# Causal attention with routed experts: keys and queries brought in on 64 partitions, high and low parts written in place

## The chip, the cores and the metric

The kernel runs on one core of a Trainium2 chip. The time is the device time of one execution in microseconds (us); the median of three runs before the change is 936.29 us (935.67 to 938.85). The trace is that of one execution.

## The reference

Attention over 8 batches x 8 heads, 576 positions, 64 values a head, followed by a two-level routed mixture of 16 experts:

```python
scores = scale * np.matmul(q, k.transpose(0, 1, 3, 2))
cum = np.cumsum(np.maximum(s, 0.0), axis=-1)
bias = -(cum[:, :, :, None] - cum[:, :, None, :])
scores = np.where(causal, -1e9, scores + np.minimum(bias, 0.0))
attn = softmax(scores)                      # row maximum subtracted
x = np.matmul(attn, v)                      # then (B*S, H*D) = (4608, 512)
g_idx = argmax(x @ w_group);  e_idx = argmax(x @ w_expert[g_idx])
out = g_w * e_w * (relu(x @ w1[g, e]) @ w2[g, e])
```

Everything is float32 to the outside. Inside, a product is made of a rounded "high" part and a "low" part, which is the value minus its high part.

## The kernel before

**Tiles.** The 64 heads are worked in 32 pairs. For a pair p there are three kinds of operand tiles. A raw tile `r` holds keys and queries of both heads, transposed: 128 partitions (64 of head 0, 64 of head 1), then key or query, then 576 positions. `WA` (four of them, in turn) holds the high parts with 64 partitions for the head's values and four more rows: two with the cumulated bias (L179) and two with the negated row maximum, high and low (L248); it has room for both heads side by side in the free dimension. `WB` (five in turn) holds on 128 partitions what the low-part products need: low keys over high keys, high queries over low queries. The constants KA = 0 and QA = 1 pick keys or queries.

**The path of a pair.** `load_raw` brings the raw tile in (576 KB). `split` rounds it on ACT into a staging tile `hl` (L152, 128x576 for keys, then the same for queries); the low parts are a subtraction (L156) on POOL, on DVE for pair 0: two of 64x576 for the keys, straight into WB, and one of 128x576 for the queries, into `hl`. `load_a` copies from `hl` to WA by DMA, once a head (L177), and adds the bias rows (L179); `load_b` copies from `hl` to WB, two DMAs a head (L189, L190). So a pair needs six on-chip copies. For pairs 0 to 2 `place` (L168) writes some of them with ACT instead.

**The loop.** A step works on one head. `rowmax` (letter A) multiplies queries by keys (L214) for the head four steps ahead, and DVE reduces each block to row maxima (L222); when both heads of a pair are done, `shift_rows` (letter T) turns the ten columns of maxima by a transposition on TensorE (L236), and `shifts` (t) makes a negated high and low part of them on DVE (L242, L243), which two DMAs from ACT's queue put into WA (D, L248). `scores` (B) makes two matmuls per block (L269 with WA, L271 with WB); ACT takes exponentials (L279, b); POOL zeroes what lies above the diagonal (L288, e), four selections a head. `av` (C) multiplies by the values (L309) for the head before, and ACT evicts (L313, L316, v). The letters Y, Z, W, K normalise, X, L, M make high and low parts of the finished output (L367, L371), O and o send it out. R steps the router.

**What sets the order.** The order on TensorE, DVE, ACT and POOL is written out by hand: the strings ORDER0 (steps −4 to 0), FIRST (steps 1 and 2) and ORDERS (from step 3) are walked letter by letter. A, B and C issue the numbered piece of that head's work, the other letters pop one entry of a first-in-first-out list. G pops one low part, S one split. `need(k, i)` pops everything of list k up to pair i. The start is by hand on SP too; from step 1 on SP's transfers are placed by the planner. `pre` lists extra calls after the early steps.

**The start.** The sums of s are scanned on DVE into `ch` (L469 to L473) and go to WA by L179. `Router` prepares constants on POOL, and `operands` makes eight conversions on DVE after step −1 (L670 to L678). The expert stage follows attention; its weight tiles take SBUF room that attention's tiles leave.

Of the kernel before, what the change touches and what calls it, by code (L numbers as in the profile page):

```python
# [8 lines left out]
F32 = mybir.dt.float32  # L9
F32R = mybir.dt.float32r  # L10
# [10 lines left out]
P = 128  # L21
# [87 lines left out]
def attention(tc, qk, v, s, wr, xs, st):  # L109
# [3 lines left out]
    with ExitStack() as ctx:  # L113
# [28 lines left out]
        hls, raws = {}, {}  # L142
        def load_raw(p):
            raws[p] = raw.tile([P, 2, S], F32, name=f"r{p}", tag="r", bufs=2)
            nc.sync.dma_start(raws[p], qk[p])

        def split(p, part, later=False):

            if part == 0:
                hls[p] = raw.tile([P, 3, S], F32R, name=f"hl{p}", tag="hl", bufs=3)  # L150
            hl, r = hls[p], raws[p]
            nc.scalar.copy(hl[:, part], r[:, part])  # L152

            def low(h):
                hr = slice(0, P) if part else slice(h * 64, h * 64 + 64)
                (nc.vector if p < 1 else nc.gpsimd).tensor_tensor(  # L156
                    out=hl[:, 2] if part else WB[p % NBB][0:64, KA, h], in0=r[hr, part],
                    in1=hl[hr, part].bitcast(F32), op=ALU.subtract)

            for h in range(1 if part else 2):  # L160
                if later:
                    push("G", p, lambda h=h: low(h))
                else:
                    low(h)

        def place(p, part):

            nc.scalar.copy(*((WA[p][0:64, :, 0, QO:], raws[p][0:64]) if part == 0 else  # L168
                             (WB[p][0:64, QA, 0], raws[p][0:64, 1]) if part == 1 else
                             (WB[p][64:128, KA, 1], raws[p][64:128, 0])))  # L170

        def load_a(p, placed=False):
            w = WA[p % NA]
            hl = hls[p].bitcast(F32)
            for h in range(2):
                if h or not placed:
                    nc.sync.dma_start(w[0:64, :, h, QO:].bitcast(F32), hl[h * 64:h * 64 + 64, 0:2])  # L177
                n = 2 * p + h
                nc.sync.dma_start(w[64:66, KA, h, QO:].bitcast(F32), (cumh if p < 4 else cumd)[n:n + 1].bitcast(F32))  # L179

        def load_b(p, placed=False):
            w = WB[p % NBB].bitcast(F32)
            hl = hls.pop(p).bitcast(F32)
            for h in range(2):

                hr = slice(h * 64, h * 64 + 64)
                b = slice(1 if placed and h else 0, 2)
                if h or not placed:
                    nc.sync.dma_start(w[0:64, QA, h], hl[hr, 1])  # L189
                nc.sync.dma_start(w[64:128, b, h], hl[hr, 0::2][:, b])  # L190
# [41 lines left out]
        def shift_rows(p):  # L232
            need("a", 2 * p + 1)
            i = p % NA
            pt = ring(f"pmt{p}", "t", True)
            nc.tensor.transpose(pt[:10, :P], mc[p % 2], ident)  # L236
            push("t", p, lambda: shifts(p, i, pt))

        def shifts(p, i, pt):
            th = sm.tile([10, P], F32R, name=f"th{p}", tag="th", bufs=1)  # L240
            tl = sm.tile([10, P], F32R, name=f"tl{p}", tag="tl", bufs=1)
            nc.vector.tensor_scalar(out=th, in0=pt[:10, :P], scalar1=-1.0, scalar2=None, op0=ALU.mult)  # L242
            nc.vector.scalar_tensor_tensor(out=tl, in0=pt[:10, :P], scalar=-1.0, in1=th.bitcast(F32), op0=ALU.mult,  # L243
                                           op1=ALU.subtract)
# [214 lines left out]
        load_raw(0)  # L459
        load_raw(1)  # L460
        wr_f = ac.tile([P, 4, 20], F32, name="wr_f")
# [46 lines left out]
        place(2, 1)
        place(2, 2)
# [22 lines left out]
        ORDER0 = "B0 b e A0 a T t B1 b D A1 a B2 b e A2 a B3 b e e A3 a B4 b e A4 a A5 a".split()  # L532
        for step in range(-LEAD, NH + 5):
# [19 lines left out]
            if step >= 2 and step // 2 + 4 < NP:  # L553
                push("S", step // 2 + 4, lambda p=step // 2 + 4, part=step % 2: split(p, part, True))
# [24 lines left out]
            if step % 2 == 1 and 0 < step < NH:  # L579
                for f, lead in ((load_a, 4), (load_b, 3), (load_v, 1), (load_raw, 6)):  # L580
                    if step // 2 + lead < NP and (f != load_v or step > 1):
                        need("S", step // 2 + lead)
                        if f in (load_b, load_raw):
                            need("G", step // 2 + lead - 2 * (f == load_raw))
                        f(step // 2 + lead)
# [39 lines left out]
class Router:  # L625
# [42 lines left out]
    def operands(self):  # L668
        V, ni, n1 = self.tc.nc.vector, self.ni, self.n1
        V.tensor_copy(self.wr_sb[:, :, 0:20], self.wr_f)  # L670
        V.tensor_tensor(out=self.wr_sb[:, :, 32:52], in0=self.wr_f, in1=self.wr_sb[:, :, 0:20].bitcast(F32),
                        op=ALU.subtract)
        V.tensor_copy(self.ub, self.uf)
        V.tensor_copy(self.ob, self.onesf)
        V.tensor_scalar(out=ni, in0=n1, scalar1=6, scalar2=None, op0=ALU.arith_shift_right)
        V.tensor_copy(self.part[:, 0], ni)
        V.tensor_scalar(out=ni, in0=n1, scalar1=63, scalar2=None, op0=ALU.bitwise_and)
        V.tensor_copy(self.part[:, 1], ni)  # L678
# [918 lines left out]
```

## Time and profile before

| | |
|---|---|
| median of three runs | 936.29 us |
| the profiled execution | 940.03 us, span 938.2 us, mean granted TensorE clock 0.981 |
| TensorE matmul busy | 872.6 us (93%) |
| DVE, ACT, POOL busy | 698.0 (74%), 607.6 (65%), 613.8 (65%) |
| DMA over the span | 174.66 MB, 186 GB/s |

Busy shares are means over the whole span: attention fills about the first 440 us, the expert stage the rest. A granted clock of 1.00 is 2.4 GHz, 0.50 is 1.2 GHz. In a timeline row, the number in front is the start in us from the span's begin, the next the duration, and the bracket says how long the engine was idle before and what ended that. A DMA issue stands on the queue (SPq, ACTq) that issues it, and its duration is that of the issue, not of the transfer.

### The profile page before, as it was taken

The numbers are of one execution on the slowest core, as the hardware profiler recorded it, in microseconds if no ns is written. First come the engines' busy times: TensorE is split into PE (matmuls) and PEld (weight loads), VectorE is DVE, ScalarE is ACT, GpSimd is POOL, SyncE is SP. The second block draws the span as 40 slices with busy tenths as digits, with TensorE's granted clock in tenths as the row PEclk, the third lists the DMA queues.
The fourth block names the chain that finished last, engine by engine and source line by source line (L and its number), as shares of the span: only waits on it lengthen the run. The fifth ranks groups of instructions, "written<-read, shape, count | busy, mean of one in ns | idle before, by whom it ended". The sixth has DMA issues, their size and how long they took to land. (4 is left out here: it accounts for less than half of the span.)

```text
span 938.2 us, 17960 instructions
## 1 busy us (share of the span) xinstructions
PE 872.6 (93%) x5648; PEld 783.8 (84%) x5648; DVE 698.0 (74%) x1986; ACT 607.6 (65%) x1382; POOL 613.8 (65%) x731
## 2 busy tenths in 40 slices
PE   4879999999999999999799999999999999999993
PEld 3768788787878788787597999899999999999992
DVE  7536586886868586886477678998888899888830
ACT  5547777776777677766646467566676666766740
POOL 9636665666757565633688556666768778878750
PEclk9979999999999999999799999999999999999997
DMA  6999988788889878733365545455554556655510
GB/s 181 233 183 222 235 221 225 181 220 210 226 197 225 211 211 217 164 98 130 123 210 183 173 162 193 157 195 209 184 189 182 204 188 226 225 203 188 195 44 23
DMA packets 80502, 174.66 MB, mean 186 GB/s; under 512 B 9580, under 2 KB 42988, under 8 KB 72208
## 3 DMA queue, kind: packets, MB, share of 16 engines
q1 hardware_dynamic: 70496, 153.52, 58.3%
q0 software_dynamic: 7488, 18.89, 5.6%
q10 hardware_dynamic: 2416, 1.03, 0.5%
q8 instruction: 47, 0.77, 0.4%
q14 instruction: 55, 0.45, 0.2%
HBM read 108.97 MB, written 19.69 MB: 137 GB/s over the span
## 5 line engine op out<-in xcount | busy, mean ns | idle before, releaser
L995 POOL TENSOR_TENSOR wl<-raw,wh 128x512 fp32r<-128x512 f32 x182 | 233.5, 1304 | 58.2 <-ACT wh L992 39.7
L222 DVE CUSTOM_DVE_ANT_0 mx<-pm,mask 128x192 bf16<-128x192 f32 (+4 forms) x320 | 129.4, 421 | 50.2 <-PE pm L214 46.1
L992 ACT CAST wh<-raw 128x512 fp32r<-128x512 f32 x256 | 153.8, 616 | 3.7 <-issue 3.1
L1093 PE MATMUL ph<-xl,wh 128*128 128x256 f32 (+13 forms) x512 | 145.5, 304 | 4.4 <-DVE xl L1065 4.1
L1093 PE MATMUL ph<-xh,wh 128*128 128x256 f32 (+13 forms) x512 | 144.4, 301 | 1.2 <-ACT xh L1064 1.1
L214 PE MATMUL pm<-WA 66*128 66x288 f32 (+4 forms) x384 | 126.8, 359 | 18.6 <-DMA WA<-ch 9.7
L269 PE MATMUL ps<-WA 68*128 68x320 f32 (+4 forms) x384 | 136.9, 360 | 6.0 <-DVE tl L243 3.0
L309 PE MATMUL po<-pt,VT 128*128 128x256 f32 (+3 forms) x512 | 123.8, 359 | 2.6 <-issue 2.1
L1148 PE MATMUL py<-hl,wh 128*128 128x256 f32 (+13 forms) x448 | 113.5, 302 | 1.3 <-DVE hl L1089 1.3
L1148 PE MATMUL py<-hh,wh 128*128 128x256 f32 (+13 forms) x448 | 112.9, 302 | 0.0
L271 PE MATMUL ps<-WB 128*128 128x320 f32 (+4 forms) x384 | 111.6, 303 | 0.0
L309 PE MATMUL po<-pu,VT 128*128 128x320 f32 (+1 forms) x384 | 108.9, 393 | 0.0
L1194 DVE STREAM_TRANSPOSE yr<-yT 32x384 f32<-32x384 f32 (+1 forms) x208 | 104.4, 502 | 4.2
L288 POOL TENSOR_SCALAR_AFFINE_SELECT pt<-pt 128x128 f32<-128x128 f32 (+2 forms) x192 | 64.2, 343 | 65.0 <-ACT pt L279 62.3
L1060 DVE STREAM_TRANSPOSE xt<-xg 32x256 f32<-32x256 f32 (+1 forms) x208 | 102.4, 493 | 3.2
L1093 PEld LDWEIGHTS ph<-xl,wh 128*128 128x128 f32 x512 | 96.7, 189 | 8.2 <-DVE xl L1065 6.2
L309 PEld LDWEIGHTS po<-pt,VT 128*128 128x128 f32 x512 | 89.0, 195 | 16.7 <-issue 3.3
L1093 PEld LDWEIGHTS ph<-xh,wh 128*128 128x128 f32 x512 | 96.8, 189 | 2.8 <-ACT xh L1064 2.4
L371 POOL TENSOR_TENSOR xTl<-xT,xTh 128x512 fp32r<-128x512 f32 x30 | 38.2, 1272 | 90.9 <-ACT xTh L367 74.3
L214 PEld LDWEIGHTS pm<-WA 66*128 66x128 f32 (+1 forms) x384 | 70.0, 195 | 32.2 <-DVE mc L222 14.9
L1088 ACT ACTIVATE hh<-ph 128x256 fp32r<-128x256 f32 (+13 forms) x128 | 53.6, 419 | 65.1 <-PE ph L1093 64.2
L156 POOL TENSOR_TENSOR WB<-r,hl 64x576 fp32r<-64x576 f32 x62 | 87.2, 1406 | 5.1 <-ACT hl L152 2.6
(230 smaller groups left out, 1994.3 us busy)
## 6 DMA issues: line engine op xcount, KB each, us to landing
raw<-in_w_dram SPq DMA_DIRECT2D x64, 1024.0 KB
r<-in_qk_dram SPq DMA_DIRECT2D x32, 576.0 KB
WA<-hl SPq DMA_DIRECT2D x61, 288.0 KB
WB<-hl SPq DMA_DIRECT2D x61, 288.0 KB
VT<-in_v_dram SPq DMA_DIRECT2D x32, 384.0 KB
WB<-hl SPq DMA_DIRECT2D x64, 144.0 KB
xs<-xr SPq DMA_DIRECT2D x15, 512.0 KB
WA<-cumd SPq DMA_DIRECT2D x56, 4.5 KB
```

The source lines that it names most:

```text
L156: (nc.vector if p < 1 else nc.gpsimd).tensor_tensor(out=hl[:, 2] if part else WB[p % NBB][0:64, KA, h], in0=r[hr, part], in1=hl[hr, part]. ...
L214: nc.tensor.matmul(ps[:rows, :cw], WA[i][0:66, QA, h, QO + q0:QO + q0 + rows], WA[i][0:66, KA, h, QO + c0:QO + c0 + cw], start=True, stop= ...
L222: nc.vector.tensor_tensor_reduce(out=tmp[:rows, :cw], in0=ps[:rows, :cw], in1=mk[:rows], scale=1.0, scalar=-3.0e38 if c0 == 0 else mo, op0 ...
L269: nc.tensor.matmul(ps[:rows, o:o + w], WA[i][0:68, KA, h, QO + k0:QO + k0 + rows], WA[i][0:68, QA, h, QO + q0:QO + q0 + w], start=True, st ...
L271: nc.tensor.matmul(ps[:rows, o:o + w], WB[p % NBB][:, KA, h, k0:k0 + rows], WB[p % NBB][:, QA, h, q0:q0 + w], start=False, stop=True)
L309: nc.tensor.matmul(po[0][:, qa - base:qb - base], VT[p % NVT].rearrange("p t a d -> p (t a d)")[:, (3 * t + 1 + h) * 64:][:, 0:P], x[:, c: ...
L992: self.casts.append(nc.scalar.copy(h[:, j], raw[:, j]))
L995: self.low = nc.gpsimd.tensor_tensor(out=l[:, j], in0=raw[:, j], in1=h[:, j].bitcast(F32), op=ALU.subtract)
L1060: V.transpose(dst[:, 0:n, :, j], src[:, 0:n, :, i])
L1093: self.product = nc.tensor.matmul(pss[f][:, :cap], w[f // 4][:, c, (f % 4) * P:(f % 4 + 1) * P], x[:, c, :cap], start=(c == 0 and w is sel ...
L1148: self.product = nc.tensor.matmul(pss[c][:, :cap], w[2 + f // 4][:, f % 4, c * P:(c + 1) * P], x[:, f, :cap], start=(f == 0 and w is self. ...
L1194: V.transpose(dst[:, 0:n, :, i], src[:, 0:n, :, j])
```

## The change

Keys and queries are laid out in HBM so that a pair's raw tile has 64 partitions, then head, key or query, and position. ACT rounds one head's keys and queries (64x1152) straight into WA; POOL (DVE for pair 0) makes four low parts of 64x576 a pair, straight into WB; two DMAs from WA to WB (288 KB each) give the high parts there. The staging tile and `place` are gone. Raw tiles have three buffers instead of two, and are loaded at even steps behind `need("G")`. The bias rows of both heads come by one DMA from pair 3 on. The ten columns of maxima are copied beside themselves on DVE, twenty are transposed, and the second DVE instruction makes the high part in ten rows and the low part in the other ten by a per-row factor (`less`, 0 or −1), so that one DMA sends them. `operands` is cut into four pieces after steps 1 to 4. Loads of values, of raw tiles and of WB move from odd steps to even ones.

```diff
-        def load_raw(p):
-            raws[p] = raw.tile([P, 2, S], F32, name=f"r{p}", tag="r", bufs=2)
-            nc.sync.dma_start(raws[p], qk[p])
+        def load_raw(p, heads=((0, 2),)):
+            raws[p] = raw.tile([64, 2, 2, S], F32, name=f"r{p}", tag="r", bufs=3)
+            for a, b in heads:
+                nc.sync.dma_start(raws[p][:, a:b], qk[p][:, a:b])
-        def split(p, part, later=False):
...
-            nc.scalar.copy(hl[:, part], r[:, part])
+        def split(p, h, later=False):
+            r, w, wb = raws[p], WA[p % NA], WB[p % NBB]
+            nc.scalar.copy(w[0:64, :, h, QO:], r[:, h])
+            def low(a):
                 (nc.vector if p < 1 else nc.gpsimd).tensor_tensor(
+                    out=wb[64 * a:64 * a + 64, a, h], in0=r[:, h, a], in1=w[0:64, a, h, QO:].bitcast(F32),
+                    op=ALU.subtract)
+            for a in (KA, QA):
                 if later:
+                    push("G", p, lambda a=a: low(a))
...
+        def load_a(p):
             w = WA[p % NA]
+            if p < 3:
...
+            else:
+                nc.sync.dma_start(w[64:66, KA, :, QO:].bitcast(F32), cumd[2 * p:2 * p + 2].rearrange("h a s -> a h s"))
+        def load_b(p):
+            w, wb = WA[p % NA].bitcast(F32), WB[p % NBB].bitcast(F32)
+            nc.sync.dma_start(wb[0:64, QA], w[0:64, QA, :, QO:])
+            nc.sync.dma_start(wb[64:128, KA], w[0:64, KA, :, QO:])
...
+            nc.vector.tensor_copy(mc[p % 2][:, 2 * NB:], mc[p % 2][:, 0:2 * NB])
             pt = ring(f"pmt{p}", "t", True)
-            nc.tensor.transpose(pt[:10, :P], mc[p % 2], ident)
+            nc.tensor.transpose(pt[:20, :P], mc[p % 2], ident)
...
+            nc.vector.scalar_tensor_tensor(out=t, in0=th.bitcast(F32), scalar=less, in1=pt[:20, :P], op0=ALU.mult,
                                            op1=ALU.subtract)
...
+                nc.scalar.dma_start(WA[i][66:68, QA].bitcast(F32).rearrange("a h q -> a (h q)"), t.bitcast(F32))
...
-        load_raw(0)
+        load_raw(0, ((0, 1), (1, 2)))
         load_raw(1)
+        load_raw(2)
...
-        place(0, 0)
         split(0, 0)
+        load_a(0)
         split(0, 1)
-        load_a(0, True)
+        load_b(0)
         split(1, 0)
+        load_a(1)
         split(1, 1)
...
+        load_raw(3)
+        load_b(1)
         rt = Router(tc, ac, late, end, kept, ring, wr_f, wr_sb, xs, st)
...
+        split(2, 0, True)
+        split(2, 1, True)
         ones(3)
...
-        pre = {-2: [(load_a, 2, True), (load_raw, 3), (load_v, 0)],
-               -1: [(load_b, 1, True), (load_raw, 4)],
-               0: [(split, 3, 0), (split, 3, 1), (load_a, 3), (load_v, 1)],
-               1: [(split, 4, 0), (split, 4, 1), (load_b, 2, True), (load_raw, 5)]}
+        pre = {-3: [(load_v, 0), (load_a, 2)],
+               -2: [(load_raw, 4)],
+               -1: [(load_b, 2)],
+               0: [(need, "G", 2), (load_raw, 5), (split, 3, 0, True), (split, 3, 1, True), (load_a, 3), (load_v, 1)],
+               1: [(load_b, 3), (need, "G", 3), (load_raw, 6)]}
...
-            if step >= 2 and step // 2 + 4 < NP:
-                push("S", step // 2 + 4, lambda p=step // 2 + 4, part=step % 2: split(p, part, True))
+            n = step // 2 + (4 if step % 2 else 3)
+            if step > 0 and n < NP:
+                push("S", n, lambda n=n, h=1 - step % 2: split(n, h, True))
...
+            if 1 <= step < 5:
+                rt.operands(step - 1)
...
+            if 0 < step < NH:
+                for f, lead in ((load_a, 4),) if step % 2 else ((load_v, 1), (load_b, 3), (load_raw, 6)):
+                    n = step // 2 + lead
+                    if n < NP:
+                        need("S", n if f != load_raw else n - 3)
+                        if f == load_raw:
+                            need("G", n - 3)
+                        f(n)
```

One G is added to the odd string of ORDERS, and four G to ORDER0.

## Rows read from the trace of the kernel before

**Rows 1.** Busy time by stretches: start and end in us, length, then for TensorE, its weight loads, DVE, ACT and POOL the busy us with the number of instructions, the granted clock, the mean busy share of the 16 DMA engines, GB/s.

```profile
2.00:6.00 4.00, 0.00 (x0) 0.00 (x0) 1.99 (x2) 0.61 (x1) 3.90 (x17) 1.00 0.96 289
20.00:30.00 10.00, 8.15 (x28) 5.96 (x28) 8.53 (x36) 2.20 (x6) 5.76 (x9) 1.00 1.01 289
30.00:50.00 20.00, 18.85 (x94) 15.52 (x93) 9.28 (x39) 12.85 (x31) 16.02 (x23) 1.00 0.95 200
50.00:55.00 5.00, 1.97 (x11) 1.74 (x11) 0.47 (x2) 0.00 (x0) 0.10 (x1) 1.00 0.95 200
55.00:70.00 15.00, 11.77 (x45) 10.02 (x46) 5.97 (x20) 8.45 (x20) 5.46 (x9) 0.66 1.06 183
70.00:85.00 15.00, 14.82 (x92) 12.53 (x90) 10.28 (x41) 11.91 (x31) 10.43 (x18) 1.00 1.02 196
243.30:295.64 52.34, 50.68 (x323) 42.44 (x322) 39.92 (x156) 39.05 (x97) 34.12 (x52) 1.00 0.88 211
```

**Rows 2.** Timeline of DVE: the instruction of L242, once a pair, from the second pair on.

```profile
25.91 0.27 DVE L242 TENSOR_SCALAR th<-pmt 10x128 fp32r<-10x128 f32 x1
40.36 0.28 DVE L242 TENSOR_SCALAR th<-pmt 10x128 fp32r<-10x128 f32 x1 [0.82 <-PE pmt L236]
57.04 0.28 DVE L242 TENSOR_SCALAR th<-pmt 10x128 fp32r<-10x128 f32 x1 [5.63 <-PE pmt L236]
74.43 0.28 DVE L242 TENSOR_SCALAR th<-pmt 10x128 fp32r<-10x128 f32 x1 [0.98 <-PE pmt L236]
86.00 0.28 DVE L242 TENSOR_SCALAR th<-pmt 10x128 fp32r<-10x128 f32 x1 [0.99 <-PE pmt L236]
97.60 0.28 DVE L242 TENSOR_SCALAR th<-pmt 10x128 fp32r<-10x128 f32 x1 [0.98 <-PE pmt L236]
112.20 0.28 DVE L242 TENSOR_SCALAR th<-pmt 10x128 fp32r<-10x128 f32 x1 [0.99 <-PE pmt L236]
...
428.05 0.28 DVE L242 TENSOR_SCALAR th<-pmt 10x128 fp32r<-10x128 f32 x1 [1.53 <-PE pmt L236]
```

**Rows 3.** Timeline of all engines, 45 to 57 us.

```profile
45.17 0.36 SPq L145 DMA_DIRECT2D r<-in_qk_dram  x1
...
55.30 0.67 ACT L152 CAST hl<-r 128x576 fp32r<-128x576 f32 x1 [6.46 <-DMA r<-in_qk_dram]
...
56.62 0.38 PE L236 MATMUL pmt<-ident,mc 128*10 128x128 f32 x1 [4.36 <-ACT pt L279]
```

**Rows 4.** Timeline of the start: the last low part of pair 0 on DVE, the first row maximum, the first row maximum of pair 1, the first score, and the first and the last of the router's eight instructions.

```profile
9.34 0.76 DVE L156 TENSOR_TENSOR hl<-r,hl 128x576 fp32r<-128x576 f32 x1
...
10.39 0.46 DVE L222 CUSTOM_DVE_ANT_0 mx<-pm,mask 128x288 bf16<-128x288 f32 x1 [0.29 <-PE pm L214]
...
16.72 0.46 DVE L222 CUSTOM_DVE_ANT_0 mx<-pm,mask 128x288 bf16<-128x288 f32 x1 [1.07 <-PE pm L214]
...
21.91 0.55 PE L269 MATMUL ps<-WA 68*128 68x256 f32 x1 [0.29 <-DMA WA<-tl]
...
22.45 0.77 DVE L670 CAST wr_sb<-wr_f 128x80 fp32r<-128x80 f32 x1
...
25.44 0.18 DVE L678 CAST part<-ni 128x40 f32<-128x40 int32 x1
```

**Rows 5.** Instructions that read or write the raw tile, and those of the shift rows, with the least, median and greatest duration in ns, the first and last start in us, and their forms.

```profile
L152 ACT CAST hl<-r x64: 657/658/674, 7.1 to 392.4; 128x576 fp32r<-128x576 f32 x64
L156 POOL TENSOR_TENSOR WB<-r,hl x62: 1395/1406/1423, 11.7 to 390.5; 64x576 fp32r<-64x576 f32 x62
...
L168 ACT CAST WA<-r x3: 1152/1152/1152, 6.0 to 15.7; 64x1152 fp32r<-64x1152 f32 x3
L156 DVE TENSOR_TENSOR WB<-r,hl x2: 751/752/754, 7.8 to 8.5; 64x576 fp32r<-64x576 f32 x2
...
L242 DVE TENSOR_SCALAR th<-pmt x32: 274/279/281, 17.1 to 428.0; 10x128 fp32r<-10x128 f32 x32
L248 ACTq DMA_DIRECT2D WA<-th x32: 722/722/1342, 17.4 to 429.6; - x32
```

**Rows 6.** What TensorE's matmuls waited for between 100 and 400 us: us in total, times, the longest.

```profile
PE pm L214 <- DVE mc L222: 3.9, 12, 0.4
PE ps L269 <- DVE tl L243: 2.5, 5, 0.5
PE ps L269 <- ACT pu L279: 2.0, 6, 0.3
PE po L309 <- POOL pt L288: 0.5, 1, 0.5
```

**Rows 7.** DMA issues between 243.30 and 295.64 us, four pairs: number and KB of each.

```profile
WA<-hl SPq DMA_DIRECT2D x8, 288.0 KB
r<-in_qk_dram SPq DMA_DIRECT2D x4, 576.0 KB
WB<-hl SPq DMA_DIRECT2D x8, 288.0 KB
VT<-in_v_dram SPq DMA_DIRECT2D x4, 384.0 KB
WB<-hl SPq DMA_DIRECT2D x8, 144.0 KB
xs<-xr SPq DMA_DIRECT2D x2, 512.0 KB
```

**Rows 8.** POOL: the first causal selection in the timeline; then, from the page's list of groups, the selections on `pt` and the low parts of finished outputs (number, busy us, mean ns, idle before).

```profile
25.08 0.28 POOL L288 TENSOR_SCALAR_AFFINE_SELECT pt<-pt 128x128 f32<-128x128 f32 x1
...
L288 POOL TENSOR_SCALAR_AFFINE_SELECT pt<-pt 128x128 f32<-128x128 f32 (+2 forms) x192 | 64.2, 343 | 65.0 <-ACT pt L279 62.3
...
L371 POOL TENSOR_TENSOR xTl<-xT,xTh 128x512 fp32r<-128x512 f32 x30 | 38.2, 1272 | 90.9 <-ACT xTh L367 74.3
```

**Rows 9.** Timeline of TensorE: the first score matmul of step 1 and that of step 2.

```profile
29.19 0.32 PE L269 MATMUL ps<-WA 68*64 68x64 f32 x1
...
37.31 0.43 PE L269 MATMUL ps<-WA 68*64 68x64 f32 x1
```

More of the change, by code (lines that the diff above doesn't have):

```diff
@@ L141, in attention @@
             nc.gpsimd.memset(t[64:P, PC[4]:PC[4] + 64], 0.0)
-        hls, raws = {}, {}
-        def load_raw(p):
-            raws[p] = raw.tile([P, 2, S], F32, name=f"r{p}", tag="r", bufs=2)
-            nc.sync.dma_start(raws[p], qk[p])
-        def split(p, part, later=False):
-            if part == 0:
-                hls[p] = raw.tile([P, 3, S], F32R, name=f"hl{p}", tag="hl", bufs=3)
-            hl, r = hls[p], raws[p]
-            nc.scalar.copy(hl[:, part], r[:, part])
-            def low(h):
-                hr = slice(0, P) if part else slice(h * 64, h * 64 + 64)
+        raws = {}
@@ L158, in low @@
-                    in1=hl[hr, part].bitcast(F32), op=ALU.subtract)
-            for h in range(1 if part else 2):
+                    out=wb[64 * a:64 * a + 64, a, h], in0=r[:, h, a], in1=w[0:64, a, h, QO:].bitcast(F32),
+                    op=ALU.subtract)
+            for a in (KA, QA):
                 if later:
-                    push("G", p, lambda h=h: low(h))
+                    push("G", p, lambda a=a: low(a))
                 else:
[L164 to L170, printed above, removed]
@@ L172, in load_a @@
-        def load_a(p, placed=False):
-            w = WA[p % NA]
[L174 to L190, printed above, removed]
+                    low(a)
@@ new lines, in load_a @@
+        def load_a(p):
+            w = WA[p % NA]
+            if p < 3:
+                for h in range(2):
+                    n = 2 * p + h
+                    nc.sync.dma_start(w[64:66, KA, h, QO:].bitcast(F32), cumh[n:n + 1].bitcast(F32))
+            else:
[4 more added lines that the diff above has]
+            nc.sync.dma_start(wb[64:128, KA], w[0:64, KA, :, QO:])
@@ L483, in attention @@
                                 compare_op=ALU.is_ge, fill=-8.0e9, base=0, channel_multiplier=1)
-        mc = [ac.tile([P, 10], F32, name=f"mc{i}") for i in range(2)]
+        mc = [ac.tile([P, 4 * NB], F32, name=f"mc{i}") for i in range(2)]
         for i in range(2):
             nc.gpsimd.memset(mc[i], 0.0)
+        less = ac.tile([20, 1], F32, name="less")
+        nc.gpsimd.memset(less, -1.0)
+        nc.gpsimd.memset(less[0:10], 0.0)
         make_identity(nc, ident)
@@ L569, in attention @@
                 f(*args)
-            if step == -1:
+            if step == -3:
                 nc.sync.dma_start(cumd, cumh.bitcast(F32))
-                rt.operands()
+            if 1 <= step < 5:
+                rt.operands(step - 1)
             if step == 62:
@@ L578, in attention @@
                 manual.enter_context(tc.manual_schedule(engines={ENG.PE, ENG.DVE, ENG.Activation, ENG.Pool}))
[L579 to L585, printed above, removed]
+            if 0 < step < NH:
[6 more added lines that the diff above has]
+                        f(n)
         for _ in range(3):
@@ L666, in __init__, with operands @@
         self.n1, self.ni, self.uf, self.onesf = n1, ni, uf, onesf
-    def operands(self):
+    def operands(self, i):
         V, ni, n1 = self.tc.nc.vector, self.ni, self.n1
[L670 to L678, printed above, removed]
+        if i == 0:
+            V.tensor_copy(self.wr_sb[:, :, 0:20], self.wr_f)
+            V.tensor_tensor(out=self.wr_sb[:, :, 32:52], in0=self.wr_f, in1=self.wr_sb[:, :, 0:20].bitcast(F32),
+                            op=ALU.subtract)
+        elif i == 1:
+            V.tensor_copy(self.ub, self.uf)
+            V.tensor_copy(self.ob, self.onesf)
+        else:
+            op, by = ((ALU.arith_shift_right, 6), (ALU.bitwise_and, 63))[i - 2]
+            V.tensor_scalar(out=ni, in0=n1, scalar1=by, scalar2=None, op0=op)
+            V.tensor_copy(self.part[:, i - 2], ni)
     def step(self, now=False):
```

27 lines of the change are left out of this document (5 added, 22 removed), and 2 rows, old and new, of the table ORDERS.

## The prediction

> **What bounds the kernel now.** Read first the table of stretches [rows 1], because the shares on the page are means over unlike stages. In the settled attention (243.30 to 295.64 us) TensorE is busy 50.68 of 52.34 us, ACT 39.05, POOL 34.12, and the 16 DMA engines are busy 0.88: TensorE sets the pace, and DMA is close behind it. From 20 to 85 us it is otherwise: the DMA share is 0.95 to 1.06 in each row, TensorE does 1.97 us of work in the 5 us from 50, and the granted clock falls to 0.66 (a mean of its two levels, 2.4 and 1.2 GHz) from 55 to 70.
>
> Next, the pace. One DVE instruction (L242) runs once per pair of heads, so its start times are milestones [rows 2]; I call them T1, T2 and so on, T0 being the first pair's. Undisturbed, with little routing work yet, a pair takes 11.57 and 11.60 us (74.43 to 86.00 to 97.60); settled it takes (428.05 − 112.20)/24 = 13.16. But the first three gaps are 14.45, 16.68 and 17.39 us: 48.52 in sum, where three undisturbed pairs take 34.8. So 13.7 us are lost between T1 and T4.
>
> Why, is read in the timeline of that stretch [rows 3]. A raw load is issued at 45.17 us and its cast starts on ACT at 55.30, after ACT sat idle 6.46 us until that DMA landed. Exponentials were queued behind this cast, and TensorE lost 4.36 us at 56.62 waiting for one of them. So the data path of keys and queries (load, cast, on-chip copies) is late while the DMA engines are full, and the instruction that waits for it blocks everything else.
>
> **Part 1: the copies.** In the settled stretch four pairs issue eight WA copies of 288 KB, eight WB copies of 288 and eight of 144 [rows 7]: 1440 KB a pair, beside 576 KB of raw loads. The change leaves two copies of 288: 576 KB. The remaining 64-partition copies move at no less than 183 GB/s if priced by the 55–70 row, and the 128-partition loads at 289 by the 2–6 row (both at a share near 1) [rows 1]. A pair then needs (0.59 + 0.59 MB)/183 + (0.39 V + 0.26 output)/289 = 6.4 + 2.3 = 8.7 us of a pace of 11.6: a share of 0.75 instead of 1. The raw loads are also issued earlier: three buffers instead of two, so pair 5 is loaded once pair 2's four low parts are done (about 28 us, part 4), not at 45; it is wanted at about 45. So the 6.46 us wait of ACT goes, and the loss between T1 and T4 with it, unless something else is late.
>
> A page speaks against this. The Trainium skill, "SBUF — State Buffer", section "Door 1: the DMA port swizzle (why [64,N] ≈ [32,N])", says that a transfer on partitions 0 to 63 reaches only 8 of the 16 ports, and so moves at half the rate of one on 128. The trace leans the same way (289 GB/s where whole-height loads run, 183 where half-height copies dominate). By the page the raw load would take twice 576 KB/289 = 4.1 us of the engines instead of 2.0. Its consequence is a rival below.
>
> **Part 2: ACT.** Two casts a pair stay, now 64x1152 at 1152 ns (that form runs in the start) instead of 128x576 at 658 [rows 5]: +0.99 us a pair. One of the two DMA issues of 722 ns on its queue goes: −0.72. That is +0.27 a pair, on an engine busy 75%. What matters is a cast's length, since an exponential or an eviction behind it waits 0.49 us longer, twice a pair. From 0.49 at full cost to nothing (hidden in ACT's idle time): 0 to 27.7 us over the 28 pairs from T4. Against that, all TensorE waits for other engines from 100 to 400 us are 8.9 us, of which ACT is named for 2.0 and the shift rows' DVE work for 2.5 [rows 6]; the shorter shift path could give some of it back, so the lower end is −8.9. I take +1.3 (those 2.0 grown by two thirds), near the rows of today. In-place writing also makes ACT wait until TensorE has read the tile four pairs back; by the order of pops that read was issued a whole step before, so no wait.
>
> **Part 3: DVE.** One copy of 10 columns a pair: no row has it; nearest is L242's 0.28 [rows 5], so 0 to 0.28, and it lies ahead of the transposition that is popped some matmuls later: 0 taken, bounds 0 to 9 us in all. In the start the first pair's low parts are four of 0.75 instead of three, and the first row maximum follows right behind at 10.39 [rows 4]: +0.3. The router's eight preparing instructions (22.45 to 25.62, 3.17 us) stood between the last row maximum of the lead and T1; now they are spread over four later steps, where DVE is busy 76%: −3.1 here and 0 there (up to +3.1 if none hides). The 1.07 us for which DVE waited at 16.72 goes as well, because pair 1 needs no copy into WA any more. T1 comes at 25.91 + 0.3 − 3.1 − 1.0 ≈ 22.1; TensorE starts scores at 21.91 today, after its own lead work, so I allow 22.3: **−3.6 us**.
>
> **Part 4: POOL.** Four low parts a pair of 1.41 us instead of three [rows 5]: +1.4, 34.12 of 52.34 becomes 39.7, 76%. Settled, that hides. At the start it may not: POOL's queue ahead of the first causal selection ends at 25.08 [rows 8], and gets two more low parts (pairs 1 and 2): 27.9. From there until T4, six heads need 6 × 4 selections of 0.343 = 8.2 us, fourteen low parts 19.7, two low parts of finished outputs 2.5: 30.4, so POOL is done at 58.3. T4 lies at 22.3 + 34.8 = 57.1 without any loss. POOL thus becomes nearly as late as TensorE; four low parts (5.6 us) come in a bunch at the end of steps 1 and 2, ahead of the selections that the next step's first product needs. I allow 2 us (bounds 0 and 6: nothing, or 2 us in each of three steps) and 3 us for the low clock, at which step 1 ran 8.1 us today (29.19 to 37.31, [rows 9]) where half of 11.6 is undisturbed. T1 to T4: 34.8 + 5 = 39.8 instead of 48.5: **−8.7 us**.
>
> **Part 5: the rest.** The queue of SP issues five transfers fewer a pair; it waits for TensorE today, so 0. Everything after T4 moves up with it: weights are loaded only when attention's tiles come free, and the expert stage starts from there. 0, with ±1.5 for a changed layout.
>
> **Sum.** −3.6 − 8.7 + 1.3 = −11.0. The profiled execution took 940.03 (938.2 of span, 1.8 around): 929.0 in such an execution. The median of the runs shown is 936.29, 3.7 less, so **925.3**.
>
> **Rivals.** (a) POOL takes DMA's place in the first steps: three steps wait 2 us each instead of 2 in all, and settled pairs lose a little more to its low parts: 925.3 + 4 + 2 = **931.3**. For it: the tally above, 58.3 against 57.1. Against: TensorE waits for POOL only 0.5 us from 100 to 400.
> (b) Half-height loads keep the DMA engines full; T1 to T4 stays at 48.5, only the start's 3.6 is won: 936.29 − 3.6 + 1.3 = **934.0**. For it: 183 against 289 GB/s. Against: even at half of 289 the pair needs 4.1 + 3.2 + 2.3 = 9.6 us of 11.6, and the loads are issued some 17 us earlier. This is where the port rule of the Trainium skill would lead.
> (c) Slower: ACT's longer cast is felt by TensorE at its full 0.49 us each time, twice a pair over 28 pairs, by the ring of three score buffers that ACT empties: +27.7 against −12.3, **951.7**. It decides from 12.3/56 = 0.22 us a cast. For it: ACT's work and eight issues of 0.722 fill 39.05 + 5.8 = 44.8 of 52.34 us. Against: the casts of 0.66 cost TensorE hardly anything today (2.0 us in 300).
> (d) The early loss is not due to the late load but to the low clock and returns elsewhere: about 936. The 4.36 us wait speaks against it.
>
> **How the numbers follow.** Forecast 0.62, (a) 0.19, (b) 0.06, (c) 0.07, (d) 0.06. The forecast's own range is 918.3 (no POOL or clock allowance, 2 us won settled) to 930. To hold 8 in 10 the range takes in (a) and stops short of (b): 918.3 to 933.5. A measurement tells 0.3%, 2.8 us, from no change: faster below 933.5 (forecast, (a), part of (b)) 0.84, same 0.09, slower 0.07.
>
> **What would show it.** The gaps T1–T2, T2–T3, T3–T4 near 13 each; T1 near 22; no wait of a cast for a raw load after 20 us; DMA share near 0.75 early and 0.66 (8.7 of 13.16) settled; settled pairs at 13.2. Wrong: a settled pair over 13.4 (ACT), selections starting late behind low parts with TensorE waiting (POOL), or a DMA share still near 1.

## The result and the profile after

The changed kernel takes 947.96 us (median of four runs, 943.96 to 948.69) where the kernel before took 935.98 beside it: a ratio of 1.0117, 95% interval [1.0078, 1.0156]. It is slower by some 12 us; the forecast was 925.3. Ten further runs gave 947.76. The profiled execution took 943.96 us (span 942.1), the fastest of the four.

The milestones come first. In the timeline of DVE, the instruction that answers to L242 in [rows 2] is L230 in the changed kernel (start in us, duration):

```profile
30.10 0.28 DVE L230 TENSOR_SCALAR th<-pmt 20x128 fp32r<-20x128 f32 x1 [0.48 <-PE pmt L224]
46.44 0.28 DVE L230 TENSOR_SCALAR th<-pmt 20x128 fp32r<-20x128 f32 x1 [0.45 <-PE pmt L224]
58.64 0.28 DVE L230 TENSOR_SCALAR th<-pmt 20x128 fp32r<-20x128 f32 x1 [1.16 <-PE pmt L224]
70.96 0.28 DVE L230 TENSOR_SCALAR th<-pmt 20x128 fp32r<-20x128 f32 x1 [0.78 <-PE pmt L224]
...
107.80 0.28 DVE L230 TENSOR_SCALAR th<-pmt 20x128 fp32r<-20x128 f32 x1 [0.91 <-PE pmt L224]
434.53 0.28 DVE L230 TENSOR_SCALAR th<-pmt 20x128 fp32r<-20x128 f32 x1 [1.45 <-PE pmt L224]
```

Set beside [rows 2] these say where the time went, stretch by stretch: T1 comes at 30.10 instead of 25.91 (4.2 us lost); T1 to T4 takes 40.86 instead of 48.52 (7.7 won); by T7 the changed kernel is 4.4 us ahead, 107.80 against 112.20. Then it loses: (434.53 − 107.80)/24 = 13.614 us a pair instead of 13.160, 10.9 us over 24 pairs. What follows T31 is 942.1 − 434.53 = 507.6 us, beside 510.1.

The stretches that answer to [rows 1] (same columns):

```profile
2.00:6.00 4.00, 0.00 (x0) 0.00 (x0) 2.23 (x3) 0.87 (x2) 3.90 (x15) 1.00 1.03 223
20.00:30.00 10.00, 4.92 (x15) 3.00 (x15) 5.41 (x27) 0.38 (x1) 8.30 (x9) 1.00 0.85 194
30.00:50.00 20.00, 17.85 (x81) 15.38 (x80) 10.80 (x40) 12.09 (x24) 9.40 (x16) 1.00 0.40 92
55.00:70.00 15.00, 13.95 (x85) 11.60 (x83) 11.95 (x42) 12.02 (x27) 13.33 (x19) 1.00 0.70 157
243.30:295.64 52.34, 48.78 (x313) 40.71 (x312) 40.05 (x151) 40.63 (x93) 38.15 (x53) 1.00 0.61 139
```

The DMA engines are mostly free now: 0.40 to 0.85 in the stretches shown after 20 us, where they were at 0.95 to 1.06 (only from 50 to 55 us is the share 1.02), and 0.61 settled (0.88 before). The clock no longer falls between 55 and 70 us. Yet TensorE does 48.78 us of work in the settled 52.34, not 50.68: it waits for something that is not a transfer. What, is told by the waits of TensorE's matmuls between 100 and 400 us, as in [rows 6]:

```profile
PE pmt L224 <- DVE mc L222: 10.6, 11, 1.0
PE pm L201 <- DVE mc L209: 7.6, 18, 0.6
PE ps L256 <- ACT pu L266: 2.0, 6, 0.3
```

The first line is new. L222 is the added copy of ten columns on DVE, L224 the transposition behind it; ACT's 2.0 us are unchanged. The instructions by duration (ns: least, median, greatest), as in [rows 5]:

```profile
L222 DVE COPY mc<-mc x32: 149/270/1143, 19.0 to 432.9; 128x10 f32<-128x10 f32 x32
...
L155 POOL TENSOR_TENSOR WB<-r,WA x124: 1389/1407/1454, 12.0 to 409.9; 64x576 fp32r<-64x576 f32 x124
...
L152 ACT CAST WA<-r x64: 1137/1140/1159, 5.7 to 404.9; 64x1152 fp32r<-64x1152 f32 x64
```

A copy of ten columns takes 149 ns at best and up to 1143. One of the long ones, in the timeline of all engines:

```profile
230.56 1.40 POOL L155 TENSOR_TENSOR WB<-r,WA 64x576 fp32r<-64x576 f32 x1
...
230.87 1.13 DVE L222 COPY mc<-mc 128x10 f32<-128x10 f32 x1
...
232.14 0.27 PE L224 MATMUL pmt<-ident,mc 128*20 128x128 f32 x1 [0.92 <-DVE mc L222]
```

The copy begins 0.31 us into a low part on POOL and ends at 232.00, 0.04 us after that low part's end (231.96). TensorE stands for 0.92 us. A hypothesis follows: DVE's copy can't run while POOL subtracts, so it takes as long as the rest of the low part. The Trainium skill, "SBUF — State Buffer", section "Who interferes with whom", states such a rule: DVE and GpSimd share a pair of SBUF ports as an exclusive lock, which a DVE `copy` can need, a DVE operation with both inputs in SBUF also does against GpSimd's reads, and a `tensor_reduce` on trn2 never does. The rows above agree with the clause on `copy` (1.13 us beside a low part, 0.149 at best); the experiments below try the other two.

### The profile page after: what moved, and what is told of

Same layout as the page of the kernel before. It is cut to its first block, busy times and chain, and to the rows that moved or that the text cites. A ratio compares the mean times of both kernels' runs of the same rounds, so it can differ in the third digit from the quotient of the medians.

```text
span 942.1 us, 17644 instructions
## 1 busy us (share of the span) xinstructions
PE 863.2 (92%) x5648; PEld 776.5 (82%) x5648; DVE 714.9 (76%) x2019; ACT 629.9 (67%) x1373; POOL 660.4 (70%) x764
## 3 DMA queue, kind: packets, MB, share of 16 engines
q10 hardware_dynamic: 1840, 1.02, 0.4%
## 5 line engine op out<-in xcount | busy, mean ns | idle before, releaser
L155 POOL TENSOR_TENSOR WB<-r,WA 64x576 fp32r<-64x576 f32 x124 | 174.7, 1409 | 10.1 <-PE pm L201 4.8
L296 PE MATMUL po<-pt,VT 128*128 128x256 f32 (+3 forms) x512 | 121.0, 353 | 0.4 <-issue 0.3
L296 PE MATMUL po<-pu,VT 128*128 128x320 f32 (+1 forms) x384 | 105.2, 381 | 0.0
L275 POOL TENSOR_SCALAR_AFFINE_SELECT pt<-pt 128x128 f32<-128x128 f32 (+2 forms) x192 | 68.3, 368 | 47.7 <-ACT pt L266 43.5
L266 ACT ACTIVATE pt<-ps 128x256 f32<-128x256 f32 (+2 forms) x192 | 75.9, 397 | 30.8 <-PE ps L258 20.9
```

The source lines that it names most:

```text
L155: (nc.vector if p < 1 else nc.gpsimd).tensor_tensor(out=wb[64 * a:64 * a + 64, a, h], in0=r[:, h, a], in1=w[0:64, a, h, QO:].bitcast(F32), ...
L296: nc.tensor.matmul(po[0][:, qa - base:qb - base], VT[p % NVT].rearrange("p t a d -> p (t a d)")[:, (3 * t + 1 + h) * 64:][:, 0:P], x[:, c: ...
```

## The experiments

The settled pace is read from each kernel's own milestones, (T31 − T7)/24. Two profiles of the changed kernel give 13.614 and 13.620, so it tells 0.02 us a pair; the time up to T7 varies more (107.80 and 110.92). In six of the profiles the granted clock falls for a few us between T7 and T31, and the pairs in which it falls are 0.4 to 2.7 us longer. The kernel before is one of them, `s_late` has two such pairs (columns as in [rows 1]):

```profile
321.73:337.23 15.50, 14.52 (x88) 11.91 (x86) 10.94 (x49) 9.92 (x26) 8.39 (x13) 0.89 0.65 154
```

```profile
158.67:174.16 15.49, 14.50 (x88) 11.89 (x86) 11.04 (x48) 10.87 (x26) 9.83 (x14) 0.89 0.45 103
213.30:230.19 16.89, 15.91 (x88) 13.18 (x86) 11.14 (x48) 11.03 (x25) 9.86 (x14) 0.80 0.44 103
```

The pairs otherwise repeat in fours. So "full clock" is the mean pair over those groups of four (T7 to T11, T11 to T15 and so on) in which the granted clock stays at 1.00. The runs were made in groups, each beside its own runs of the kernel before (medians 936.59, 939.78, 935.54 and 935.06), so across groups the ratios are to be compared. "xT" is the mean of DVE's product `xT<-vals,st` (128x576, both inputs in SBUF) between 107 and 420 us.

| kernel | median us | ratio to before, 95% | T1 | T7 | pair | full clock | xT us |
|---|---|---|---|---|---|---|---|
| before | 936.59 | | 25.91 | 112.20 | 13.160 | 13.095 | 0.942 |
| after | 947.96 | 1.0117 [1.0078, 1.0156] | 30.10 | 107.80 | 13.614 | 13.614 | 1.025 |
| after_again | 947.76 | 1.0092 [1.0065, 1.0119] | 31.82 | 110.92 | 13.620 | 13.620 | 1.026 |
| rows_old | 938.07 | 1.0018 [0.9985, 1.0051] | 28.57 | 104.71 | 13.371 | 13.371 | 1.254 |
| copy_reduce | 940.30 | 1.0022 [0.9994, 1.0050] | 31.37 | 107.77 | 13.394 | 13.364 | 1.058 |
| before_copy | 944.53 | 1.0080 [1.0042, 1.0119] | 27.31 | 114.00 | 13.382 | 13.382 | 0.817 |
| low_cut | 934.03 (one) | | 29.23 | 104.64 | 13.258 | 13.258 | 1.055 |
| cast_cut | 935.16 (one) | | 29.01 | 104.58 | 13.310 | 13.261 | 1.133 |
| start_a | 940.23 | 1.0027 [0.9999, 1.0055] | 31.55 | 107.68 | 13.474 | 13.376 | 1.257 |
| start_b | 938.80 | 0.9999 [0.9973, 1.0026] | 29.71 | 107.22 | 13.387 | 13.373 | 1.253 |
| k_rows_old | 945.50 | 1.0101 [1.0058, 1.0144] | 28.42 | 105.50 | 13.623 | 13.623 | 1.111 |
| k_before | 950.46 | 1.0162 [1.0117, 1.0206] | 25.61 | 109.38 | 13.615 | 13.615 | 1.099 |
| low_wait | 931.38 | 0.9959 [0.9935, 0.9982] | 28.95 | 105.99 | 13.085 | 13.085 | 0.959 |
| s_late | 940.82 (one) | | 28.32 | 105.36 | 13.478 | 13.301 | 0.965 |

**Is it the copy?** Four kernels, `after_again` being the changed one itself. `rows_old` goes back to ten columns, without the copy and with two DMAs for the shift rows; `before_copy` adds the copy and twenty columns to the kernel before; `copy_reduce` writes the same ten columns by another operation:

```diff
-            nc.vector.tensor_copy(mc[p % 2][:, 2 * NB:], mc[p % 2][:, 0:2 * NB])
+            nc.vector.tensor_reduce(out=mc[p % 2][:, 2 * NB:], in_=mc[p % 2][:, 0:2 * NB].unsqueeze(2),
+                                    axis=AX.X, op=ALU.max)
```

> The changed kernel once more, with another profile. The profiled execution of 943.96 us was its fastest of four; the others took 947.8 to 948.7 at a mean granted clock of 0.984 instead of 0.993. Expected: 947 to 949 us, settled pairs (T7 to T31) at 13.6 us again, and some 4 us more in stretches with a low clock, at the start or between attention and experts.

> The changed kernel with the row shifts of before: ten columns, no DVE copy, two DMAs. Theory L (TensorE's transposition waits for the DVE copy, which POOL's low parts make long): settled pairs go from 13.61 back to 13.15 us, the time falls by 11 to about 937; T1 to T7 change by 1 to 2 us at most. Theory C (the casts of 1.15 us on ACT hold TensorE) and theory P (POOL's fourth low part a pair): settled pairs stay at 13.5 to 13.6, the time at 946 to 948.

> The changed kernel with the copy of ten columns written as a maximum over an axis of length one: the same place, operands and result, another DVE operation. Theory L with a lock (the copy form waits while POOL works, the reduction does not): L222 takes about 0.15 to 0.2 us each time instead of 0.15 to 1.14, settled pairs 13.2, time about 939. Theory L as a mere extra link in the chain: L222 as long as before, settled pairs 13.5 to 13.6. Theories C and P: no change, 947.

> The kernel before with one thing added: the DVE copy of ten columns in front of the transposition, and twenty columns transposed (the second ten unused). Theory L: settled pairs rise from 13.16 to 13.4 or 13.6, the time by 6 to 11 us to 942 to 947. Theories C and P: 936 to 937, no change.

Without the copy 9.7 us are back (938.07 beside 947.76), and 0.243 us a pair. With the maximum over an axis of one, which writes the same values, nearly as many (940.30, 7.5 us), and 0.250 us a pair at full clock. By duration, in `copy_reduce`:

```profile
L222 DVE TENSOR_REDUCE mc<-mc x32: 141/157/159, 18.8 to 427.6; 128x10 f32<-128x10 f32 x32
```

It never takes longer than 159 ns, beside low parts that begin and end as in the changed kernel, and the wait of the transposition for it is gone. So in the settled pairs it is not the link in the chain that costs, but the kind of operation in it: the lock. And the copy is just as dear where nothing else is changed. In `before_copy`:

```profile
L235 DVE COPY mc<-mc x32: 150/169/1260, 17.7 to 433.6; 128x10 f32<-128x10 f32 x32
```

Its pair goes from 13.095 at full clock to 13.382, with 10.3 us of waits between 100 and 400 us of the transposition for this copy, which were not there before.

**What is left.** `rows_old` still needs 13.371 us a pair, 0.276 more than before at full clock: 6.6 us over 24 pairs, which eat up most of the 7.5 us won by T7. Two suspects: ACT's casts of 1.14 us, or POOL's fourth low part. `low_cut` leaves out, from pair 5 on, 512 of the 576 columns of the fourth low part; `cast_cut` leaves out, from pair 5 on, ACT's rounding of the queries. Two more kernels, on the same base, shift the raw loads of the start; they follow below.

```diff
+                c = 64 if p >= 5 and a == QA and h == 1 else S
...
-                    out=wb[64 * a:64 * a + 64, a, h], in0=r[:, h, a], in1=w[0:64, a, h, QO:].bitcast(F32),
+                    out=wb[64 * a:64 * a + 64, a, h, 0:c], in0=r[:, h, a, 0:c],
...
```

```diff
-            nc.scalar.copy(w[0:64, :, h, QO:], r[:, h])
+            if p < 5:
+                nc.scalar.copy(w[0:64, :, h, QO:], r[:, h])
+            else:
+                nc.scalar.copy(w[0:64, KA, h, QO:], r[:, h, KA])
```

> The changed kernel with the row shifts of before (no copy), and from pair 5 on the fourth low part (queries of the second head) done for 64 of its 576 columns only; it leaves out part of the computation (the rest of that low part stays that of an earlier pair). GpSimd loses about 1.2 us a pair. Theory P (GpSimd's low parts hold VectorE's operation with two inputs in SBUF, xT<-vals,st, and so the chain of the pairs): settled pair 13.37 -> 13.16 to 13.20 us, xT back from 1.23 towards 0.95 us. Theory C (ScalarE's casts of 1.15 us bound the pair): settled pair stays at 13.35 to 13.40.

> The same base, and from pair 5 on ScalarE casts the keys of a pair only; it leaves out part of the computation (the high parts of the queries stay those of an earlier pair). ScalarE loses about 1.0 us a pair. Theory C: settled pair 13.37 -> 13.16 to 13.20 us. Theory P: stays at 13.35 to 13.40, with xT still at about 1.2 us.

Neither theory got its number: at full clock the two are at 13.258 and 13.261, each 0.11 below `rows_old`, where the excess is 0.276. Over the kernel before, `cast_cut`, `low_cut` and `rows_old` have 0.19, 0.11 and 0.31 us more in xT, and 0.17, 0.16 and 0.28 more in the pair. That is only a hint, for `copy_reduce` has 0.12 and 0.27. So I looked for what xT meets, in the timeline of `rows_old`:

```profile
323.36 1.40 POOL L155 TENSOR_TENSOR WB<-r,WA 64x576 fp32r<-64x576 f32 x1 [0.82 <-ACT WA L152]
323.43 1.95 DVE L341 TENSOR_TENSOR xT<-vals,st 128x576 f32<-128x576 f32 x1
```

Undisturbed, xT takes 0.76 us. In one pair of every four it begins 0.04 to 0.10 us after a low part and takes 1.92 to 1.98; in the other three it takes 0.76, 1.13 and 1.19, as in the kernel before. In `cast_cut` the low part begins 0.5 us earlier against xT, so xT takes 1.43 to 1.47 there. In `low_cut`, which shortens another low part, it still takes 1.93 in that pair, but 0.79 and 0.76 where it took 1.19 and 1.13. Theory X: such contacts are the rest of the loss, and the new one in every fourth pair is all of the difference to before.

The single pairs bear this out better than their mean. Here is one that begins at T19, with its xT, in the kernel before and in `rows_old`; then four pairs in a row, from T19 to T23:

```profile
269.40 0.28 DVE L242 TENSOR_SCALAR th<-pmt 10x128 fp32r<-10x128 f32 x1 [0.99 <-PE pmt L236]
274.24 0.76 DVE L354 TENSOR_TENSOR xT<-vals,st 128x576 f32<-128x576 f32 x1
283.24 0.28 DVE L242 TENSOR_SCALAR th<-pmt 10x128 fp32r<-10x128 f32 x1 [0.42 <-PE pmt L236]
```

```profile
265.07 0.28 DVE L229 TENSOR_SCALAR th<-pmt 10x128 fp32r<-10x128 f32 x1 [0.99 <-PE pmt L223]
269.91 1.98 DVE L341 TENSOR_TENSOR xT<-vals,st 128x576 f32<-128x576 f32 x1
280.09 0.28 DVE L229 TENSOR_SCALAR th<-pmt 10x128 fp32r<-10x128 f32 x1 [0.41 <-PE pmt L223]
```

| kernel | four pairs, us | xT in them, us |
|---|---|---|
| before | 13.84, 12.41, 12.19, 13.90 | 0.76, 1.19, 1.13, 0.76 |
| rows_old | 15.02, 12.41, 12.20, 13.89 | 1.98, 1.19, 1.13, 0.76 |
| cast_cut | 14.50, 12.41, 12.18, 13.90 | 1.44, 1.20, 1.13, 0.76 |
| low_cut | 14.97, 12.00, 12.14, 13.90 | 1.93, 0.79, 0.76, 0.76 |

The first pair is longer by what xT takes longer, to within 0.05 us, and the three others are those of before to 0.01 in `rows_old`. `low_cut` leaves that collision alone; what it wins, it wins in the second pair, with an xT shorter by 0.40 (in the third, 0.37 less is worth only 0.05).

**A move that was no clean test.** The first try gave xT a head start, by popping its entry (K) right behind the transposition (W), ahead of one small row maximum; `k_before` does the same to the kernel before:

```diff
-            "W e A4 C5 e C6 b a A5",
+            "W K e A4 C5 e C6 b a A5",
```

> The changed kernel with the row shifts of before, and VectorE's xT<-vals,st of a pair issued straight behind the second transposition st<-rc, ahead of one 64x64 row maximum (at present behind it). In one pair of four this operation begins 0.07 to 0.10 us after a low part on GpSimd and takes 1.92 to 1.98 us instead of 0.76. Theory X (the settled loss that is left without the copy is this one collision: over three kernels the pair's excess goes with the mean of xT): begun 0.25 us earlier it takes 0.76 us in that pair, mean 0.76 to 0.95, settled pair 13.37 -> 13.10 to 13.20 us, the whole 938.1 -> 931 to 934. Rival (theory C or P by plain busy time): xT becomes short, the settled pair stays at 13.33 to 13.40 and the whole at 937 to 939.

> The kernel before with the same one move. Its xT takes 0.76 us in two pairs of four and 1.12 to 1.19 in the others (none 1.9). Theory X: little to win, settled pair 13.16 -> 13.05 to 13.16 us, the whole 0 to 3 us shorter. Rival (the move helps by itself, whatever the low parts do): as much won as in the changed kernel, 4 to 7 us.

Both became slower, `k_before` by 1.6%. In that pair of four xT did get its 0.76 us, and then it was the low part that was held (`k_rows_old`):

```profile
328.02 0.76 DVE L341 TENSOR_TENSOR xT<-vals,st 128x576 f32<-128x576 f32 x1
328.07 1.97 POOL L155 TENSOR_TENSOR WB<-r,WA 64x576 fp32r<-64x576 f32 x1 [0.82 <-ACT WA L152]
```

The low part takes 1.97 us instead of 1.41: who begins first holds the other. But in the three other pairs xT now runs into more of POOL's work (1.32, 1.51 and 0.90 us), and in every pair a row maximum, and with it a row-maximum buffer, now comes 0.8 to 1.5 us later. TensorE waits 12.1 us for row maxima between 107 and 420 us instead of 9.1, and ACT 19.4 us for TensorE's scores instead of 5.2. In the kernel before, where no xT takes 1.9 us, the move costs even more (13.095 to 13.615 us a pair). The move has a price of its own that hides what it was to show.

**A wait on the engine that has time.** In `rows_old` POOL is idle for 3.61 us after the low part that collides. So `low_wait` delays that one, the first of each pair, until xT is done; nothing on DVE, ACT or TensorE is moved. `s_late` gets there by another way: ACT's cast is issued one pop later (`v S` for `S v` in the order of odd steps).

```diff
-                (nc.vector if p < 1 else nc.gpsimd).tensor_tensor(
+                i = (nc.vector if p < 1 else nc.gpsimd).tensor_tensor(
...
+                if h == 0 and a == KA and st.xmul is not None:
+                    tc.add_manual_dep(i.ins, st.xmul.ins.name, mybir.DependencyInfo(mybir.DependencyClass.Sync,
+                                                                                  mybir.DependencyReason.DATA), reason="x")
...
-                nc.vector.tensor_tensor(out=x, in0=vals, in1=m["f"], op=ALU.mult)
+                st.xmul = nc.vector.tensor_tensor(out=x, in0=vals, in1=m["f"], op=ALU.mult)
```

> The changed kernel with the row shifts of before, and the first low part of a pair (keys of its first head) made to wait on GpSimd for the end of the xT<-vals,st that VectorE was given last; where the two collide (323.43 us and every fourth pair) GpSimd has 3.61 us idle behind that low part. Unlike the move of xT it delays nothing on VectorE. Theory X: xT 0.76 us there, mean 0.95 as before the change, settled pair 13.37 -> 13.14 to 13.22 us, the whole 938.1 -> 932 to 935, so about 2 to 4 us less than before the change. Rival (plain busy time of GpSimd and ScalarE): xT short, pair unchanged at 13.33 to 13.40, the whole 937 to 939.

> The same base, with ScalarE's cast of that step issued one pop later, behind the copy vals<-po, so that the low part begins some 2.4 us later and misses xT. Theory X: xT back to a mean of 0.95 us; the exponentials behind the cast are 0.5 us later in that step, so the settled pair lies between 13.16 and 13.37 us. Rival: pair at 13.37 or above, with xT short.

`low_wait` takes 931.38 us, a ratio of 0.9959 [0.9935, 0.9982]: less than before the change. Its timeline at the same place:

```profile
320.12 0.76 DVE L345 TENSOR_TENSOR xT<-vals,st 128x576 f32<-128x576 f32 x1
321.01 1.42 POOL L156 TENSOR_TENSOR WB<-r,WA 64x576 fp32r<-64x576 f32 x1 [1.79 <-PE pm L205]
```

The low part begins 0.13 us after xT's end (the bracket names a matmul that ended close by, and on which the low part doesn't depend). TensorE's waits between 100 and 400 us are nearly those of [rows 6] again:

```profile
PE pm L205 <- DVE mc L213: 3.9, 12, 0.4
PE ps L260 <- DVE tl L234: 3.0, 6, 0.5
PE ps L260 <- ACT pu L270: 2.0, 6, 0.3
```

The pair is at 13.085, as long as before at full clock (13.095), with casts of 1.14 us and four low parts as in the changed kernel; from T19 on the four pairs take 13.84, 12.41, 12.18 and 13.92 us. So the excess of `rows_old` was this collision and nothing that those two cost in busy time. What `low_wait` gains on the kernel before comes ahead of T7 (105.99 instead of 112.20). `s_late` frees xT as well (0.965). Its 13.478 would fit the rival, but it holds the two pairs at the lower clock shown above; at full clock it is 13.301, within theory X's range. Why it stays 0.2 above `low_wait` wasn't followed; that the later cast delays the exponentials behind it, as was expected, is argued and not shown.

**The start.** T1 came at 30.10 where 22.3 was forecast. In the timeline of TensorE (consecutive matmuls drawn together), the first row maximum and the first score of the changed kernel:

```profile
12.70 0.95 PE L201 MATMUL pm<-WA 66*128 66x288 f32 x3 [12.70 <-DMA WA<-ch]
...
27.96 0.58 PE L256 MATMUL ps<-WA 68*128 68x256 f32 x1 [3.79 <-DMA WA<-tl]
```

Both wait for a transfer of a few KB. The bias rows for the first were issued at 7.27 us and landed 5.4 us later, behind the raw loads of pairs 1 and 2; the shift rows for the second were issued at 20.49 and took some 7.4 us, while before they took 3.1 (18.84 to 21.91 in [rows 4]). Theory Q: these small transfers wait behind the raw loads, which the change issues earlier. `start_a` issues those of pairs 2 to 4 later, `start_b` also that of pair 1. Part of the edit of `start_b`:

```diff
-        load_raw(1)
-        load_raw(2)
...
+        load_raw(1)
...
-        load_raw(3)
+        load_raw(2)
...
```

> The same base, with the raw loads of pairs 2 to 4 issued later: pair 2's behind the second split of step 0, pair 3's three steps before, V's first at the end, pair 4's at step 0. Theory Q (the small rearranging DMAs of the start wait behind the raw loads on the same queues): first row-max matmul at 10 to 11 us instead of 12.7, first causal score 2 to 3 us earlier, the whole 2 to 4 us less than without (938.1 -> 934 to 936). Rival (the start is bound by the raw loads themselves, which only come later): T1 unchanged or later, 938 or more.

> As start_a, and pair 1's raw load issued behind the first high part's rearranging DMA. Theory Q: that DMA lands at about 9.5 us, the first row-max matmul at about 9.7 us, and T0 2 to 3 us earlier than in the changed kernel; whether T1 follows depends on pair 1's raw tile, which comes about 2 us later. The whole 933 to 936. Rival: the bytes ahead of T1 are the same in any order, so T1 stays and the whole is 938.

The first matmul obeys, the first score doesn't. In `start_a` and then in `start_b`:

```profile
9.81 0.95 PE L201 MATMUL pm<-WA 66*128 66x288 f32 x3 [9.81 <-POOL WA L454]
...
30.12 0.55 PE L256 MATMUL ps<-WA 68*128 68x256 f32 x1 [9.55 <-DMA WA<-tl]
```

```profile
9.24 0.95 PE L201 MATMUL pm<-WA 66*128 66x288 f32 x3 [9.24 <-DMA WA<-ch]
...
28.28 0.55 PE L256 MATMUL ps<-WA 68*128 68x256 f32 x1 [5.06 <-DMA WA<-tl]
```

The three us won at the first matmul are lost before T1 (31.55 and 29.71, against 28.57 without), as both rivals had it. But theory Q isn't refuted by that. These are the stretches from the issue of the later shift rows to the first score, in the kernel before, the changed one, `start_a` and `start_b` (columns as in [rows 1]):

```profile
18.84:21.91 3.07, 2.41 (x6) 1.42 (x7) 2.77 (x13) 0.40 (x1) 2.92 (x3) 1.00 0.79 168
```

```profile
20.49:27.96 7.47, 3.08 (x9) 1.72 (x8) 4.45 (x22) 0.00 (x0) 7.24 (x8) 1.00 0.98 231
```

```profile
21.59:30.12 8.53, 0.00 (x0) 0.03 (x1) 0.00 (x0) 0.00 (x0) 6.52 (x7) 1.00 1.02 222
```

```profile
22.42:28.28 5.86, 0.80 (x4) 0.35 (x3) 1.71 (x8) 0.39 (x1) 5.68 (x16) 1.00 1.03 234
```

The DMA share is 0.98 to 1.03 with the change and 0.79 without. The two kernels emptied the engines around the bias rows (share 0.98 in the changed kernel, 0.40 and 0.01 in these, landing after 5.4, at most 2.4 and 2.0 us) and moved the loads into the stretch of the shift rows. So full DMA engines go with the slow landing in both places, which fits theory Q, but which transfers hold the shift rows, 5.7 to 9.1 us from issue to landing in all kernels with the change, stays open: nothing was run with the copies and loads of that time left out.

## Why the prediction was wrong

The mechanism that the change aims at was read rightly, and its price elsewhere wrongly.

- **Part 1, the copies: right.** No cast waits for a raw load after 20 us. The settled DMA share is 0.61 (0.66 forecast), 0.40 from 30 to 50 us. Rival (b), DMA still full, is out: the gaps from T1 to T4 did shrink. Its mechanism shows at the start, 223 GB/s at a share of 1.03 from 2 to 6 us beside 289 before: 0.77 of the rate, not half.
- **Part 2, ACT: right in effect, a little too dear.** 1.3 us had been taken; ACT's share of TensorE's waits stayed at 2.0 us, and with the collision gone the pair is as long as before (13.085 and 13.095) although the casts take 1.14. The sign that was named for ACT, a settled pair over 13.4, did come (13.61), but from DVE. Rival (c) named a time close to the measured one (951.7) for a reason that plays no part.
- **Part 3, DVE: wrong, the first failed step.** "0 to 0.28, and it lies ahead of the transposition that is popped some matmuls later: 0 taken". The size of the copy was right (149 ns), but it isn't alone: behind a low part it takes up to 1.14 us, and TensorE waits for most of it (0.92 us in the case shown). `after` less `rows_old` is 0.243 us a pair, less `copy_reduce` 0.250: 6 us over 24 pairs; in the medians 9.7 and 7.5. By T7 `rows_old` is a further 3.1 us ahead, but `copy_reduce` (107.77) is not, so that part isn't the lock's. "Some matmuls later" was an assumption about TensorE's order; the wait of the transposition shows them too few. The upper bound of 9 was about the size, the 0 taken was not.
- **Part 4, POOL: near up to T4, in part by luck, and wrong behind it.** T1 to T4 is 40.86 us, 39.8 forecast, but in gaps of 16.34, 12.20 and 12.32, not 13 each. The 3 us for the low clock have something to them: the score matmul of 128x448 takes 0.57 us at 38.83 and 0.37 at 47.32 (before the change 0.57 at 33.98, 0.37 at 41.24), though the granted clock is given as 1.00 there. The 2 us for POOL didn't come, TensorE waits for nothing of POOL's from T1 to T4; 2.0 us of waiting for the new copy stood in their place. Behind T4, "settled, that hides" weighed only POOL's free time. The low parts have room on POOL, and yet the first of a pair, by where it falls, holds a DVE operation that TensorE's order hangs on: 13.371 less 13.085 is 0.286 us a pair, 6.9 us over 24. Rival (a) had settled pairs lose to the low parts, but 2 us in all.
- **Part 3, the start: wrong.** T1 was to be 22.3 by work on DVE; it was 30.10, 7.8 later, since the first score waits for the shift rows' transfer, which by [rows 4] took 3.1 us and which I had left as it was. In `rows_old` T1 is 28.57, in `copy_reduce`, where nothing holds the link, 31.37, so the lock isn't the reason. The DMA engines are full while that transfer is on its way, by the raw loads and copies that the change brings earlier; which of them hold it is open.
- **Part 5: right.** From T31 to the end it is 507.6 to 510.3 us in all kernels.

Sum over the profiled executions: T1 4.2 lost, T1 to T4 7.7 won, T4 to T7 0.9 won, T7 to T31 10.9 lost (12.5 at full clock), the rest 2.5 won: 4.0 longer, 943.96 against 940.03. That profile of before lay above its runs' median, and that of after below, hence 12 us between the medians. With both collisions gone, in `low_wait`, T1 to T4 takes 39.71 us (39.8 forecast), and the settled pairs cost nothing; with T1 at 28.95 instead of 22.3, 3.7 us are left of the 11.0 (931.38 beside 935.06).

## What to carry to other kernels

An operation on DVE is not priced by its size alone: ask what POOL is doing in that moment, and whether both inputs lie in SBUF or a plain copy is used. Where the two collide, choose a form that isn't held (here a maximum over an axis of one), or let the engine that has idle time behind it wait for the other: a wait that costs nothing took the ratio from 1.0018 to 0.9959 here. And work that fits into an engine's free time still needs a place where it holds nobody.

## What the runs showed that I had not expected

A DVE copy of ten columns took 0.149 us alone and up to 1.341 beside a low part on POOL (in `after_again`), a reduction of the same ten columns 0.159 at most. DVE's product of two tiles took 0.76 us alone, and 1.92 to 1.98 begun 0.04 to 0.10 us after a low part; begun 0.05 us ahead of it, it took 0.76 and the low part 1.97 instead of 1.41. And taking the first raw loads out of the way brought the first matmul 3 us earlier and the first score not at all.
